# LSH attention with a mixture of experts: whole tiles of slots, low parts on GpSimd, doubled heads with bits last, routing in seven parts

## The chip, the cores and the metric

The kernel runs on one core of a Trainium2 chip. The core has a matrix engine (TensorE, "PE" in the profile, with its weight loads shown apart as "PEld"), three engines for elementwise work (VectorE "DVE", ScalarE "ACT", GpSimd "POOL") and SyncE ("SP"), which here issues most transfers. Every engine works through its own instructions strictly in the order in which the program wrote them, and waits on semaphores for what other engines or transfers have to deliver first. The metric is the device time of one launch in microseconds (us), lower is better; the result must agree with the reference.

## The reference, cut to what matters

Two stages follow each other. The first is attention in buckets: 4 batches of 8 heads, 768 positions, 64 features per head. Six projections give six sign bits for each query and each key, and a query sees only the keys whose six bits are the same as its own. The second is a mixture of 8 experts over the 3072 positions (512 features each, 1024 hidden): every position goes to the one expert with the largest gate logit.

Shortened:

```python
q_bucket = np.sum((np.einsum('bhsd,dk->bhsk', q, proj) > 0) * powers, axis=-1)
k_bucket = np.sum((np.einsum('bhsd,dk->bhsk', k, proj) > 0) * powers, axis=-1)
mask = q_bucket[:, :, :, None] == k_bucket[:, :, None, :]
scores = np.where(mask, scale * np.matmul(q, k.transpose(0, 1, 3, 2)), -1000000000.0)
attn = np.exp(scores - np.max(scores, axis=-1, keepdims=True))
attn = attn / (np.sum(attn, axis=-1, keepdims=True) + 1e-09)
x = np.matmul(attn, v).transpose(0, 2, 1, 3).reshape(B * S, H * D)
...
logits = x @ w_gate
expert_idx = np.argmax(logits, axis=1)
gate_w = softmax(logits)[np.arange(N), expert_idx]
...
h = np.maximum(x_sorted[lo:hi] @ w1[e], 0.0)
y_sorted[lo:hi] = h @ w2[e]
...
return gate_w[:, None] * y
```

## The kernel before, in words

**Order.** No planner is at work (`manual_schedule`): each engine's instructions stand in the order in which the Python code emits them. Moving a line in the code moves it in the queue of its engine.

**Attention.** The 32 heads are taken in 16 pairs; a pair has twelve units of 128 queries by 768 keys (`unit`), so there are 192 units. The main loop runs over rounds `c`, two units per round and six rounds per pair, and is a pipeline. In round `c` TensorE does the value matmuls of round c-5 (`pv`, L339), twelve transposes of exponentials of round c-2 (`trans`, L307) and the score matmuls of round c (`score`, L271 and L273). ScalarE takes the exponentials of round c-1 (`expo`, L288) and evacuates most transposes (L329). VectorE evacuates some (L327) and takes the maxima of the scores (L278 to L280), on which the next exponentials depend.

**Scores with the mask in them.** `qk` tiles hold four planes of a head: plane 1 the rounded keys, plane 3 their low part, planes 0 and 2 the queries rounded, and 64 rows of plane 0 the queries' low part; sixteen rows of planes 2 and 3 hold the sign bits, scaled so that equal buckets add a large constant. A score is a sum of two matmuls per half of the keys, first the one of 80 rows with low parts and bits (L271), then the one of 128 rows (L273). Each head stands twice, so it is loaded into both halves of the 128 partitions (`load_x`, two transfers of 64 rows). For later pairs GpSimd splits the heads (`split`, L175 to L182), 12 pieces spread over the rounds of the pair before, and makes the bits (`lsh_bits`, L234 and L236), which go through a table in DRAM into the sixteen rows (`mask`). For the first two heads this has a form of its own: `lsh_first` (projection, L214), `split_first` (L191 and on) with copies on ScalarE, VectorE and GpSimd, and `bits_first` on VectorE (L234 and L236).

**Routing.** When the four pairs of a batch are through, `route` takes one half batch (384 positions, tiles of 128 x 24): the largest logit, the one-hot of the first expert that has it, ranks by matmuls with a triangle of ones (L421 to L426), and the slot of each position. It is a generator with ten pauses; in each round `go` runs three or two of the parts. `scatter` then writes the rows with indirect transfers of GpSimd to their slots in DRAM (L449). For the last batch the routing stands among the first expert's matmuls.

**Experts.** `pick_first` finds the expert with the most rows once three batches are counted, `rank_all` orders the others. The loads go in phases: the first expert in two halves of 256 slots, then experts with room for 456, 432, 408, 396, 384, 372 and 354 slots; rows beyond that go to a loop at the end. `rows` loads the slots of a phase in tiles of up to 128 (the last one shorter: 72, 48, 24, 12, 128, 116 and 98 rows), `xt` transposes four feature groups (L664) and splits them into a rounded and a low part (L670 and L671). `chunk_part` does the same for the weights, piece by piece of 128 x 512: for the first expert the copies alternate between GpSimd and VectorE in half of the chunks (L622) and the differences are GpSimd's (L623); for all others ScalarE copies (L625), and the differences alternate between VectorE and GpSimd (L626). `mm1` (L689) makes the hidden layer from three products of rounded and low parts, evicted by ScalarE and VectorE (L693 and L694); `mm2` (L715) or, for up to 384 slots, `yout` (L732) the output; where `mm2` is used, `yout` transposes it back (L739). VectorE weighs the rows (L741) and GpSimd scatters them to the output (L743). The weights and rows of the next phase are prepared while the present one is computed.

Of the kernel before, what the change touches and what calls it, by code (L numbers as in the profile page):

```python
# [7 lines left out]
F32 = mybir.dt.float32  # L8
# [42 lines left out]
def lsh_attention_moe(ctx, tc, qk, v, proj, wg, w1, w2, out):  # L51
# [32 lines left out]

    ones = const.tile([128, 128], BF16, name="ones")
# [10 lines left out]
    nc.sync.dma_start(wgt, wg)  # L96

    p = ps.tile([128, 512], F32, name="o")
    for _ in range(WARM):
        nc.tensor.matmul(p, ones, ones[:, None, :].to_broadcast([128, 4, 128]), start=True, stop=True)  # L100
# [83 lines left out]
    def split_first(h, half):  # L184
# [80 lines left out]
    def score(i):  # L265
# [4 lines left out]
        for a in range(2):  # L270
            nc.tensor.matmul(p[:, a, :HALF], k[0:80, 2, c], k[0:80, 3, a * HALF:(a + 1) * HALF], start=True, stop=False)  # L271
        for a in range(2):
            nc.tensor.matmul(p[:, a, :HALF], k[:, 0, c], k[:, 1, a * HALF:(a + 1) * HALF], start=False, stop=True)  # L273
# [121 lines left out]
    def route(b, hf):  # L395

        l = wk.tile([128, 2, 3, E], F32, name="rl")
# [7 lines left out]
        yield  # L405
        nc.vector.tensor_reduce(mx, lg, axis=AX.X, op=OP.max)
        yield
        nc.vector.tensor_tensor(eq, lg, bc(mx), op=OP.is_equal)
        yield
        nc.vector.tensor_tensor(eq, eq, dsc, op=OP.mult)  # L410
# [4 lines left out]
        nc.vector.tensor_tensor(oh, dsc, bc(fi), op=OP.is_equal)  # L415
        yield
        nc.vector.tensor_tensor(lg, lg, bc(mx), op=OP.subtract)
# [14 lines left out]
        nc.vector.tensor_tensor(pb, pb, oh, op=OP.mult)  # L432
# [4 lines left out]
        yield  # L437
        nc.vector.tensor_reduce(f[:, 2], ex, axis=AX.X, op=OP.add)
        yield
        nc.vector.reciprocal(XR[b, hf][:, :, GC], f[:, 2])  # L440
        SL[b, hf] = slot

# [29 lines left out]
    def pick_first():  # L472
        k = keys("key0")
        t = const.tile([128, 4], F32, name="pf")
# [300 lines left out]
    for c in range(NC + 2):  # L775
# [42 lines left out]
        for q, n in routes:  # L818
            go(q, n)
# [199 lines left out]
```

## Time and profile before

| quantity | value |
|---|---|
| time, median of 3 runs | 808.83 us (808.76 to 809.11) |
| time of the profiled execution | 808.29 us |
| its span in the trace | 806.5 us |
| instructions | 14075 |
| exponentials on ScalarE (L288) | 192, of 991 ns |
| maxima on VectorE (L278) | 192, of 952 ns |
| moved by transfers | 114.45 MB, 142 GB/s on average |

The profiled execution is one launch; its span runs from the first to the last thing that the hardware profiler recorded. In a row of the timeline stand the start in microseconds from the start of the span, the busy time, the engine, the line, the operation, the output and input by their names in the program, their shapes, how many instructions the row holds, and in brackets the idle time of the engine before the row with what ended it. In a row by stretches stand the stretch, its length, and then, for PE, PEld, DVE, ACT and POOL, the busy microseconds with the number of instructions, and at the end the granted clock of TensorE, the DMA share and GB/s. In a row of groups stand busy time and mean nanoseconds, and after a bar the idle time before and its releaser. Rows of the chain of waits give the time at which a step began, how long it lasted, engine, output and line.

### The profile page before, as it was taken

Reading aid. Unit: us, or ns where it says so; the run is one execution under the profiler, and the core shown is the slowest. Engines: PE = TensorE matmul, PEld = TensorE weight load, DVE = VectorE, ACT = ScalarE, POOL = GpSimd, SP = SyncE. Lnnn points to the kernel's source line nnn. Section 1 sums busy time; section 2 is a strip of 40 time slices with the busy share of each in tenths; the row PEclk is TensorE's granted clock in tenths of the full one; section 3 lists DMA queues with packets and bytes.
Section 4 is the critical chain, followed back from the end, with each engine's and each line's share of the span. In section 5 each row is a group of like instructions: output and inputs, shape, how many; then the busy total and the mean of one; then the engine's idle time right before and its main releaser. Section 6 shows DMA issues by size and latency. Waiting matters only on the chain.

```text
span 806.5 us, 14075 instructions
## 1 busy us (share of the span) xinstructions
PE 786.3 (97%) x4942; PEld 614.6 (76%) x4942; DVE 524.2 (65%) x1222; ACT 441.7 (55%) x879; POOL 431.1 (53%) x523
## 2 busy tenths in 40 slices
PE   7999999999999999999999989999999999999996
PEld 3767776677667766777667758988999999989894
DVE  6777777897777887778877854472564744445331
ACT  3766776766667766676666731443334343434310
POOL 5976467486756668745769263342333434345311
PEclk6999999999999999999999999999999999999999
DMA  9769963265346336433445113844444445545200
GB/s 228 187 173 282 312 176 98 67 194 160 81 119 158 95 108 202 98 79 98 130 112 164 68 53 136 270 143 161 129 146 150 147 131 175 173 154 189 86 10 35
DMA packets 47248, 114.45 MB, mean 142 GB/s; under 512 B 8265, under 2 KB 12233, under 8 KB 47176
## 3 DMA queue, kind: packets, MB, share of 16 engines
q1 hardware_dynamic: 40504, 97.18, 41.6%
q0 software_dynamic: 6672, 16.35, 6.7%
q8 instruction: 40, 0.66, 0.3%
q14 instruction: 32, 0.26, 0.1%
HBM read 87.50 MB, written 26.51 MB: 141 GB/s over the span
## 4 chain that ended last, share of the span: by engine, by line
PE 85%; DVE 5%; issue 5%; ACT 1%; DMA 1%; POOL 1%; SPq 0%; DVEq 0%; POOLq 0%; ACTq 0%
PE o L339 16%; PE t L307 15%; PE t L689 14%; PE t L715 9%; PE s L271 8%; PE s L273 8%; PE s L732 7%; DVE m L278 2%; PE t L373 2%; PE t L229 2%; PE t L356 1%; PE s L689 1%; ACT e L288 1%; PE s L739 1%; DMA xd<-in_qk_dram 1%
## 5 line engine op out<-in xcount | busy, mean ns | idle before, releaser
L288 ACT ACTIVATE e<-s,m 128x768 f32<-128x768 f32 x192 | 190.2, 991 | 130.1 <-DVE m L280 127.8
L278 DVE TENSOR_REDUCE m<-s 128x1 f32<-128x768 f32 x192 | 182.8, 952 | 62.8 <-PE s L273 54.4
L307 PE MATMUL t<-ident,e 128*128 128x128 f32 x1152 | 148.2, 278 | 1.2 <-ACT pt L329 1.0
L307 PEld LDWEIGHTS t<-ident,e 128*128 128x128 f32 x1152 | 125.4, 141 | 31.3 <-DVE m L280 10.2
L339 PE MATMUL o<-pt,vt 128*64 128x384 f32 x768 | 145.9, 502 | 0.0
L689 PE MATMUL t<-xh,w 128*128 128x456 f32 (+6 forms) x672 | 127.1, 346 | 1.1 <-DVE hh L694 1.1
L626 POOL TENSOR_TENSOR w<-raw,w 128x512 fp32r<-128x512 f32 x56 | 71.9, 1289 | 96.3 <-ACT w L625 96.1
L689 PEld LDWEIGHTS t<-xh,w 128*128 128x128 f32 x672 | 119.1, 188 | 4.4 <-DVE hh L694 1.5
L329 ACT ACTIVATE pt<-t 128x512 f32<-128x512 f32 (+1 forms) x194 | 103.6, 591 | 1.9 <-PE t L307 1.9
L339 PEld LDWEIGHTS o<-pt,vt 128*64 128x64 f32 x768 | 47.0, 137 | 59.1 <-issue 55.2
L626 DVE TENSOR_TENSOR w<-raw,w 128x512 fp32r<-128x512 f32 x56 | 55.9, 1002 | 55.0 <-ACT w L625 50.3
L743 POOL DMA_INDIRECT out_dram<-y,ix x27 | 31.3, 1159 | 92.0 <-DVE y L741 78.6
L715 PE MATMUL t<-hh,w 128*128 128x456 f32 (+3 forms) x384 | 78.9, 359 | 0.0
L327 DVE COPY pt<-t 128x512 f32<-128x512 f32 (+1 forms) x97 | 66.0, 682 | 16.2 <-PE t L307 13.8
L693 ACT ACTIVATE hh<-t 128x256 fp32r<-128x256 f32 (+7 forms) x64 | 31.4, 490 | 79.4 <-PE t L689 79.4
L715 PEld LDWEIGHTS t<-hh,w 128*128 128x128 f32 x384 | 69.8, 188 | 2.8
L694 DVE SCALAR_TENSOR_TENSOR hh<-t,hh 128x256 fp32r<-128x256 f32 (+7 forms) x64 | 35.4, 554 | 50.3 <-ACT hh L693 48.9
L625 ACT ACTIVATE w<-raw 128x512 fp32r<-128x512 f32 x112 | 66.3, 623 | 0.0
L732 PE MATMUL s<-w,hh 128*128 128x512 f32 (+2 forms) x264 | 64.5, 398 | 0.0
L271 PE MATMUL s<-qk 80*128 80x384 f32 x192 | 55.9, 372 | 3.2 <-ACT e L288 3.2
L234 POOL TENSOR_SCALAR bits<-bits 64x384 f32<-64x384 f32 x15 | 22.6, 1510 | 63.6 <-ACT bits L240 63.6
L732 PEld LDWEIGHTS s<-w,hh 128*128 128x128 f32 (+2 forms) x264 | 47.8, 185 | 11.3
(206 smaller groups left out, 1124.6 us busy)
## 6 DMA issues: line engine op xcount, KB each, us to landing
raw<-in_w_dram SPq DMA_DIRECT2D x64, 512.0 KB, 3.7
xd<-in_qk_dram SPq DMA_DIRECT2D x36, 384.0 KB, 5.4
xhe<-in_qk_dram SPq DMA_DIRECT2D x15, 768.0 KB, 8.6
w<-in_qk_dram SPq DMA_DIRECT2D x28, 384.0 KB, 5.4
sorted_rows<-xr SPq DMA_DIRECT2D x8, 1156.0 KB, 14.5
vt<-in_v_dram SPq DMA_DIRECT2D x16, 384.0 KB, 3.3
xg<-sorted_rows SPq DMA_DIRECT2D x19, 289.0 KB, 4.6
masks<-bits SPq DMA_DIRECT2D x15, 192.0 KB, 1.9
```

What stands on the lines that cost most here:

```text
L271: nc.tensor.matmul(p[:, a, :HALF], k[0:80, 2, c], k[0:80, 3, a * HALF:(a + 1) * HALF], start=True, stop=False)
L278: nc.vector.tensor_reduce(m[:, 0:1], p[:, :, :HALF], axis=AX.XY, op=OP.max)
L288: nc.scalar.activation(e, p[:, :, :HALF], AF.Exp, bias=m[:, 2:3], scale=m[:, 1:2], accum_out=SM[g, hf][:, t, s:s + 1])
L307: nc.tensor.transpose(p[:, x * 128:(x + 1) * 128], e[w][:, kt // 3, (kt % 3) * 128:(kt % 3) * 128 + 128], ident)
L327: nc.vector.tensor_copy(o, x)
L329: nc.scalar.activation(o, x, AF.Copy)
L339: nc.tensor.matmul(p[s * 64:(s + 1) * 64, :HALF], VT[g][:, kt, s, :], PT[u][:, s, kt, :], start=(kt == 0), stop=(kt == NT - 1))
L625: nc.scalar.activation(w[:, 0, a], r, AF.Copy)
L626: (nc.vector if a % 2 else nc.gpsimd).tensor_tensor(w[:, 1, a], r, w[:, 0, a], op=OP.subtract)
L689: nc.tensor.matmul(p[:, :c], w[:, a, d, fs], x[:, b, d, :c], start=(k == 0), stop=(k == 11))
L715: nc.tensor.matmul(p[:, :c], w[:, a, f % 4, ms], h[b][:, f, :c], start=(k == 0), stop=(k == 23))
L732: nc.tensor.matmul(p[:pw], HH[n][b][:, f, i:i + pw], w[:, a, f % 4], start=(k == 0), stop=(k == 23))
```

## The change

It has seven parts.

1. *Start.* A second array, in which each head stands twice, is made on the host; `load_x` brings a head with one transfer of 128 rows. The first head is loaded ahead of everything, the projection through ScalarE's queue, and the first values and the gate weights come after the loads of heads 2 and 3.
2. *Warming.* 3, 3 and 9 further matmuls without a use stand among the first ones.
3. *First scores.* The copies of `split_first` come ahead of its differences; VectorE takes the first head's queries' difference, GpSimd all differences of keys. One bits operation of head 1 comes earlier. For the first four units the matmul with low parts and bits comes second.
4. *Routing.* `route` has seven parts, two per round, at two places of a round. Comparisons are written as a difference and a comparison with zero. For the first three batches those and the products are GpSimd's. For the last batch the second half's end, the scatter and the second load of rows stand in the middle of a matmul group of the first expert (`third`).
5. *First expert.* `pick_first` has pauses and is spread over three rounds; its weights are loaded two rounds later than before. In the last two rounds `xt` comes ahead of the weights.
6. *Weights.* All copies for the first expert and all differences are GpSimd's.
7. *Tiles.* `rows`, `tokens` and `xt` take whole tiles of 128 slots, and `yout` transposes up to 72 columns where a tile was shorter.

```diff
-        nc.sync.dma_start(x[0:64], qk[h])
-        nc.sync.dma_start(x[64:128], qk[h])
+        nc.sync.dma_start(x, qk2[h])
...
+    load_x(0)
+    pj = const.tile([128, 32], F32, name="pj")
+    nc.scalar.dma_start(pj, proj)
+    load_x(1)
...
-    load_x(0)
-    pj = const.tile([128, 32], F32, name="pj")
-    nc.sync.dma_start(pj, proj)
-    load_x(1)
-    load_v(0)
...
+    def warmth(p, n):
+
+        for _ in range(n):
+            nc.tensor.matmul(p, ones, ones[:, None, :].to_broadcast([128, 4, 128]), start=True, stop=True)
...
         copy(t[:, 0, c], x[:, c])
-        nc.gpsimd.tensor_tensor(t[64:128, 0, c], x[64:128, c], t[64:128, 0, c], op=OP.subtract)
         copy(t[0:80, 2, c], x[0:80, c])
+        (nc.gpsimd if h or half else nc.vector).tensor_tensor(t[64:128, 0, c], x[64:128, c], t[64:128, 0, c],
+                                                              op=OP.subtract)
         if half == 0:
             for a in range(2):
-                (nc.gpsimd if a or h else nc.vector).tensor_tensor(
+                nc.gpsimd.tensor_tensor(
...
+        for low in ((False, True) if i < 4 else (True, False)):
+            for a in range(2):
+                n = slice(a * HALF, (a + 1) * HALF)
+                if low:
+                    nc.tensor.matmul(p[:, a, :HALF], k[0:80, 2, c], k[0:80, 3, n], start=i >= 4, stop=i < 4)
+                else:
+                    nc.tensor.matmul(p[:, a, :HALF], k[:, 0, c], k[:, 1, n], start=i < 4, stop=i >= 4)
...
+        eng = nc.gpsimd if b < B - 1 else nc.vector
...
-        nc.vector.tensor_tensor(eq, lg, bc(mx), op=OP.is_equal)
-        yield
-        nc.vector.tensor_tensor(eq, eq, dsc, op=OP.mult)
+        eng.tensor_tensor(lg, lg, bc(mx), op=OP.subtract)
+        eng.tensor_scalar(eq, lg, 0.0, None, op0=OP.is_equal)
+        eng.tensor_tensor(eq, eq, dsc, op=OP.mult)
...
-        nc.vector.tensor_tensor(oh, dsc, bc(fi), op=OP.is_equal)
-        yield
-        nc.vector.tensor_tensor(lg, lg, bc(mx), op=OP.subtract)
+        eng.tensor_tensor(eq, dsc, bc(fi), op=OP.subtract)
+        eng.tensor_scalar(oh, eq, 0.0, None, op0=OP.is_equal)
...
-        nc.vector.tensor_tensor(pb, pb, oh, op=OP.mult)
+        eng.tensor_tensor(pb, pb, oh, op=OP.mult)
...
-            (nc.vector if a % 2 and c > 1 else nc.gpsimd).tensor_copy(w[:, 0, a], r)
+            nc.gpsimd.tensor_copy(w[:, 0, a], r)
...
-            (nc.vector if a % 2 else nc.gpsimd).tensor_tensor(w[:, 1, a], r, w[:, 0, a], op=OP.subtract)
+            nc.gpsimd.tensor_tensor(w[:, 1, a], r, w[:, 0, a], op=OP.subtract)
...
-            nc.sync.dma_start(XG[n][:pw, j], xsv[bass.ds(EV[r], 1), o + i:o + i + pw].rearrange("o p w -> p (o w)"))
+            nc.sync.dma_start(XG[n][:, j], xsv[bass.ds(EV[r], 1), o + i:o + i + 128].rearrange("o p w -> p (o w)"))
...
-            nc.tensor.transpose(p[:, i:i + pw], heads(XG[n][:pw, j], d), ident[0:pw, 0:pw])
+            nc.tensor.transpose(p[:, j * 128:(j + 1) * 128], heads(XG[n][:, j], d), ident)
...
+            yw = max(pw, min(128, CAPS[1] - i))
             for m in range(4):
-                nc.tensor.transpose(p[:pw, m * 128:(m + 1) * 128], YT[n][:, m, i:i + pw], ident)
+                nc.tensor.transpose(p[:yw, m * 128:(m + 1) * 128], YT[n][:, m, i:i + yw], ident)
...
     lsh_first(0)
+    warmth(ps.tile([128, 512], F32, name="t", bufs=3), 3)
     split_first(0, 0)
...
     split_first(1, 0)
+    bits_first(1, 0)
+    warmth(ps.tile([128, 512], F32, name="t", bufs=3), 3)
 
     load_pair(1)
     load_x(2)
     load_x(3)
+    load_v(0)
+    nc.sync.dma_start(wgt, wg)
...
-        for q, n in routes:
-            go(q, n)
+        for q in routes:
+            next(q, None)
+        if c in (NC - 13, NC - 11, NC - 10):
+            next(pick)
...
-                for a in (0, 2, 3):
+                for a in (2, 3):
                     bits_first(1, a)
+                warmth(ps.tile([128, 512], F32, name="t", bufs=3), 9)
...
+            for w in routes:
+                next(w, None)
...
-        if c == NC - 11:
-            pick_first()
+        if c == NC - 9:
+            next(pick, None)
             raw_load(0, 0)
             raw_load(0, 1)
         if c == NC - 6:
             rows(0)
+        if c >= NC - 2:
+            xt(0, c - (NC - 2))
         if c >= NC - 6:
             weights((1, 1, 1, 2, 1, 2, 3, 3)[c - NC + 6])
-        if c >= NC - 2:
-            xt(0, c - (NC - 2))
...
+    def third():
+        go(last[1], 3)
+        scatter(B - 1, 1)
+        rows(1)
 
     mm1(0, 2, second)
-
     mm1(0, 3)
-    go(last[1], 9)
-    scatter(B - 1, 1)
-    rows(1)
-    for f in range(4, 8):
+    mm1(0, 4, third)
+    for f in range(5, 8):
         mm1(0, f)
```

More of the change, by code (lines that the diff above doesn't have):

```diff
@@ L89, in lsh_attention_moe @@
     nc.scalar.activation(warm, warm, AF.Exp, bias=0.0, scale=1.0)
-    load_x(0)
-    pj = const.tile([128, 32], F32, name="pj")
-    nc.sync.dma_start(pj, proj)
-    load_x(1)
-    load_v(0)
     wgt = const.tile([128, NP, 32], F32, name="wgt")
[L96 to L100, printed above, removed]
+    def warmth(p, n):
+        for _ in range(n):
+            nc.tensor.matmul(p, ones, ones[:, None, :].to_broadcast([128, 4, 128]), start=True, stop=True)
+    warmth(ps.tile([128, 512], F32, name="o"), WARM)
     def iota(shape, pattern, name, base=0, cm=0):
@@ L269, in score @@
         c = slice((3 * hf + t) * 128, (3 * hf + t) * 128 + 128)
[L270 to L273, printed above, removed]
+        for low in ((False, True) if i < 4 else (True, False)):
[5 more added lines that the diff above has]
+                    nc.tensor.matmul(p[:, a, :HALF], k[:, 0, c], k[:, 1, n], start=i < 4, stop=i >= 4)
         SC[i] = p
@@ L473, in pick_first @@
         k = keys("key0")
+        yield
         t = const.tile([128, 4], F32, name="pf")
@@ L649, in tokens @@
         IX[n] = moe.tile([128, 4], I32, name="ix", bufs=3)
-        for j, m, pw in full_and_rest(c):
-            nc.vector.tensor_copy(IX[n][:pw, j:m], XG[n][:pw, j:m, GC + 1].bitcast(I32))
+        t = len(tiles_of(c))
+        nc.vector.tensor_copy(IX[n][:, :t], XG[n][:, :t, GC + 1].bitcast(I32))
     def heads(x, d):
@@ L662, in xt @@
         p = ps.tile([128, 512], F32, name="t", bufs=3) if d % 2 or n == 0 else ps.tile([128, 512], F32, name="o")
-        for j, (i, pw) in enumerate(tiles_of(c)):
-            nc.tensor.transpose(p[:, i:i + pw], heads(XG[n][:pw, j], d), ident[0:pw, 0:pw])
+        t = len(tiles_of(c))
+        for j in range(t):
+            nc.tensor.transpose(p[:, j * 128:(j + 1) * 128], heads(XG[n][:, j], d), ident)
         if d == 0:
             GT[n] = moe.tile([128, 4], F32, name="gate", bufs=3)
-            for j, m, pw in full_and_rest(c):
-                nc.vector.tensor_copy(GT[n][:pw, j:m], XG[n][:pw, j:m, GC])
+            nc.vector.tensor_copy(GT[n][:, :t], XG[n][:, :t, GC])
             tokens(n)
@@ L760, in lsh_attention_moe @@
     load_x(3)
+    load_v(0)
+    nc.sync.dma_start(wgt, wg)
     NC = NU // 2
-    routes, parts = [], list(range(16))
+    routes, parts, pick = [], list(range(16)), pick_first()
     def weights(n):
@@ L842, in lsh_attention_moe @@
             b, q = divmod(c - 24, 24)
+            for w in routes:
+                next(w, None)
             if q == 3:
-                routes.append((route(b, 0), 3))
+                routes.append(route(b, 0))
             if q == 7:
-                routes.append((route(b, 1), 2))
+                routes[:] = [route(b, 1)]
                 scatter(b, 0)
             if q == 13:
+                routes.clear()
                 scatter(b, 1)
-        if c == NC - 11:
-            pick_first()
+        if c == NC - 9:
+            next(pick, None)
             raw_load(0, 0)
@@ L871, in lsh_attention_moe @@
     last = [route(B - 1, 0), route(B - 1, 1)]
-    go(last[0], 7)
+    go(last[0], 4)
     pv(u, 4)
@@ L878, in lsh_attention_moe @@
     lgt_ev(u, lgt(u), False)
-    go(last[0], 10)
+    go(last[0], 3)
     scatter(B - 1, 0)
```

18 lines of the change are left out of this document (7 added, 11 removed).

## The prediction

> **What bounds the kernel now.** I read the page first: its busy times, then its chain of waits.
>
> ```profile
> span 806.5 us, 14075 instructions
> PE 786.3 (97%) x4942; PEld 614.6 (76%) x4942; DVE 524.2 (65%) x1222; ACT 441.7 (55%) x879; POOL 431.1 (53%) x523
> PE 85%; DVE 5%; issue 5%; ACT 1%; DMA 1%; POOL 1%; SPq 0%; DVEq 0%; POOLq 0%; ACTq 0%
> ```
>
> TensorE works for 97% of the span and carries 85% of the chain. So another engine's work is worth something only where TensorE stops, is slowed, or streams something that need not be streamed. I therefore looked, in the timeline, for the places where TensorE has an idle time in brackets, and found five kinds of loss: the start, routing inside attention, one hole at 421 us, one at 475 us, one at 540 us. A sixth is hidden in the transposes of short tiles. Next came the table by stretches, whose last three columns are granted clock, DMA share and GB/s:
>
> ```profile
> 9.00:10.00 1.00, 1.00 (x8) 0.16 (x8) 0.97 (x2) 0.00 (x0) 0.77 (x1) 0.50 0.98 224
> 12.00:13.00 1.00, 1.00 (x5) 0.94 (x3) 0.79 (x1) 0.37 (x1) 0.92 (x1) 0.50 1.08 412
> 21.00:24.00 3.00, 3.00 (x22) 2.96 (x21) 1.48 (x4) 1.23 (x4) 2.90 (x3) 0.91 1.02 229
> 476.00:478.00 2.00, 2.00 (x12) 0.73 (x12) 0.59 (x2) 0.66 (x2) 2.00 (x3) 0.50 0.44 166
> ```
>
> While half-height head loads run, the queue moves 224 GB/s; while the 128-row loads of values and pairs run, 412. The clock is at half until about 21.5 us, and again at 476 to 478.
>
> **Start: 4.5 us.** These timeline rows carry it:
>
> ```profile
> 6.99 0.94 ACT L191 ACTIVATE qk<-xd 128x384 fp32r<-128x384 f32 x2 [4.73 <-DMA xd<-in_qk_dram]
> 10.60 0.94 ACT L191 ACTIVATE qk<-xd 128x384 fp32r<-128x384 f32 x2 [2.67 <-DMA xd<-in_qk_dram]
> 9.41 1.38 DVE L236 TENSOR_SCALAR qk<-t,thr,mul 16x384 fp32r<-16x384 f32 x2
> 12.21 0.96 DVE L278 TENSOR_REDUCE m<-s 128x1 f32<-128x768 f32 x1 [1.42 <-PE s L273]
> 16.80 0.96 DVE L278 TENSOR_REDUCE m<-s 128x1 f32<-128x768 f32 x1
> 19.23 0.83 POOL L175 CAST w<-w 128x768 fp32r<-128x768 f32 x1
> 19.52 2.48 PE L307 MATMUL t<-ident,e 128*128 128x128 f32 x12
> 25.56 0.59 PE L271 MATMUL s<-qk 80*128 80x384 f32 x2 [0.83 <-ACT e L288]
> 36.32 1.00 POOL L182 TENSOR_TENSOR w<-w,w 64x384 fp32r<-64x384 f32 x1
> 38.68 0.59 PE L271 MATMUL s<-w 80*128 80x384 f32 x2
> ```
>
> The doubled array lets one 128-row load bring a head. A head is 786 KB: 3.5 us at 224 GB/s, 1.9 at 412, so head 0 is there at 5.4 instead of 6.99, and head 1 (twice the bytes; 7.0 us or 3.8) at about 7.3 instead of 10.60. VectorE's bits of head 0 end at 10.79, 3.8 us after landing. That chain keeps its length (the subtraction that VectorE gives to GpSimd is replaced by one of 64 rows that it takes over), so the bits end at 9.2. Today four matmuls follow the bits before the first maximum can start at 12.21. With bits last, two follow, and at full clock they take some 0.5 us: maximum at 9.8, a gain of 2.4. One of head 1's bits now comes ahead of the maxima (half of a 1.38 pair is 0.7; I take 0.55, since the row-wise kind is shorter), so the third maximum moves from 16.80 by 2.95. The 18 extra warming matmuls stand where TensorE waits anyway. They should keep the granted clock up. Then the last score (0.7 after the third maximum's bits at 13.85), the next pair's projection (about 0.9) and the first twelve transposes (1.46, as in the chain rows below, not 2.48) end at about 17.0, not 22.0. After that TensorE waits on exponentials (25.56), whose inputs moved by as much as the scores. GpSimd is the limit from the other side: it starts on the next pair (19.23) when head 1 is split, some 3.2 earlier, and its last split would end at 37.3 - 3.2 = 34.1, while TensorE would want that pair at 38.68 - 4.5 = 34.2. So the bounds are 3.0 (VectorE and GpSimd) and 5.1 (TensorE). I take 4.5, nearer to the TensorE rows, since both other engines wait for it from 22 us on. Without full clock only about 2.0 remain. The projection load on ScalarE's queue shows in no row; landing like the other start loads it is hidden, and as late as head 1 it would cost 1.5. The values load, now behind the loads of heads 2 and 3, is first needed after 31 us.
>
> **Routing: 1.0 us.** The chain of waits gives the length of four groups of six rounds by their transposes:
>
> ```profile
> 132.14 1.46 PE t L307 x12
> 160.80 1.46 PE t L307 x12
> 190.07 1.46 PE t L307 x12
> 218.40 1.46 PE t L307 x12
> L408 DVE TENSOR_TENSOR rl<-rl,rf 128x24 f32<-128x24 f32 x8 | 4.9, 610 | 0.2
> ```
>
> A plain group takes 28.33 (190.07 to 218.40). The group with a batch's first route takes 28.66, which I take to be that route's matmuls alone (0.33); the one with the second 29.27, so 0.94, 0.6 more than its matmuls. Three such groups lose 1.8 us to VectorE: its 24-element comparison takes 610 ns on average, too long for so few elements. GpSimd now does these. Each result crosses between engines, and VectorE and TensorE would wait in order (behind them: the maxima, then exponentials, then scores) if GpSimd were late. By the places in the program it reaches a part about when VectorE does. Bounds 1.7 gained to 1.5 lost; I take 1.0.
>
> **Hole at 421: 1.0 us.**
>
> ```profile
> 419.12 0.16 DVE L466 TENSOR_TENSOR key<-base,base 128x8 f32<-128x8 f32 x1
> 420.94 0.66 PE L307 MATMUL t<-ident,e 128*128 128x128 f32 x4 [1.01 <-ACT pt L329]
> ```
>
> The first expert's choice is eight small VectorE operations in one round, and the evacuations queued behind them hold the transposes for 1.01 us. Spread over three rounds they fit in VectorE's idle time; bounds 0.5 and 1.2. The weight load starts two rounds (some 9 us) later and is still used only three rounds after that, so it stays hidden; SyncE queues nothing urgent behind it.
>
> **Hole at 475: 3.2 us.**
>
> ```profile
> 474.23 0.86 DVE L622 CAST w<-raw 128x512 fp32r<-128x512 f32 x1 [1.68 <-POOL w L623]
> 475.01 0.41 DVE L671 TENSOR_TENSOR xhe<-t,xhe 128x256 fp32r<-128x256 f32 x1
> 475.48 0.80 PE L689 MATMUL s<-xhe,w 128*128 128x256 f32 x2 [1.89 <-DVE xhe L671]
> 476.79 3.83 PE L339 MATMUL o<-pt,vt 128*64 128x384 f32 x16
> 183.17 1.44 PE o L339 x8
> ```
>
> VectorE's weight copy waits 1.68 us for GpSimd, and the token split that TensorE needs stands behind it. The change gives the copies to GpSimd and puts the split first: the hole goes, but for about 0.3. The clock is at half after it (the 476 row above): sixteen value matmuls take 3.83, where eight at full clock take 1.44 (the last row, from the chain), so 0.95 less; and the 1.3 us between the hole's end and them would be 0.65. Together 1.6 + 1.6 = 3.2. GpSimd's copies and differences of the last eight parts (0.63 + 1.28 each) then end near 480, as now, ahead of their use after 490. The bounds are 1.6 and 3.5.
>
> The Trainium skill ("TensorE: Matmul & The Clock Gate", Why this matters for your kernels) allows idle gaps up to about 3 us without loss of clock. Here 1.89 us were enough; by the page the half clock would have another cause, and the sum would lose 1.6.
>
> **Hole at 540: 1.2 us.**
>
> ```profile
> 532.80 6.41 DVE L626 TENSOR_TENSOR w<-raw,w 128x512 fp32r<-128x512 f32 x2
> 533.03 5.03 POOL L626 TENSOR_TENSOR w<-raw,w 128x512 fp32r<-128x512 f32 x4
> 539.81 12.76 PE L689 MATMUL t<-xh,w 128*128 128x456 f32 x60 [1.12 <-DVE hh L694]
> L626 POOL TENSOR_TENSOR w<-raw,w 128x512 fp32r<-128x512 f32 x56 | 71.9, 1289 | 96.3 <-ACT w L625 96.1
> L743 POOL DMA_INDIRECT out_dram<-y,ix x27 | 31.3, 1159 | 92.0 <-DVE y L741 78.6
> ```
>
> Two VectorE differences take 6.41 us while GpSimd does four, and the hidden-layer evictions behind them stop TensorE. With all of them on GpSimd that is gone. GpSimd gets 56 x 1.289 = 72 us more. An expert then costs it 16 x 1.29 + 4 x 1.16 = 25 us, against 34 to 44 of TensorE (only the second half of the first expert, 24.5 us, is as short). There the queue behind the last scatter ends near 541, and the weights are first used after 552.57.
>
> The Trainium skill ("GPSIMD Engine Reference", 4.1 Engine selection) says not to give two-input elementwise work to GpSimd, which is about twice as slow. Per piece the trace agrees, 1289 ns; where the cover holds it is free.
>
> **Short tiles: 2.8 us.**
>
> ```profile
> 527.35 0.56 PE L664 MATMUL o<-ident,xg 128*128 128x128 f32 x4
> 527.70 3.05 PE L732 MATMUL s<-w,hh 128*128 128x512 f32 x12
> 557.36 0.68 PE L664 MATMUL o<-ident,xg 128*128 128x128 f32 x4
> 557.97 5.22 PE L715 MATMUL t<-hh,w 128*128 128x456 f32 x24
> 641.48 0.65 PE L664 MATMUL o<-ident,xg 128*128 128x128 f32 x4
> 642.05 1.19 PE L715 MATMUL t<-hh,w 128*128 128x408 f32 x5
> ```
>
> Four transposes whose last has 72 rows take 0.35 us until the next matmul starts; with 48 rows 0.61, with 12 rows 0.57. The short ones cost 0.22 to 0.26 more though they stream less. Whole tiles should all take 0.35. Three experts (48, 24, 12 rows) with four such sets each: 4 x (0.26 + 0.23 + 0.22) = 2.8. The 72-, 116- and 98-row tiles gain nothing. If a whole tile paid for its columns instead, the term would be -0.5. Output transposes of at most 72 columns stream 128 anyway: nothing.
>
> **Sum.** 4.5 + 1.0 + 1.0 + 3.2 + 1.2 + 2.8 = 13.7. The profiled execution took 808.29 (its span and 1.8 around it), so 794.6; the median of the runs shown lies 0.5 higher, and I forecast 795.1.
>
> **Rivals.** *The start is worth half*: the clock falls back or GpSimd's splits set the pace. For: GpSimd is busy 2.90 of 3 us there; against: its last split has 1.3 us to spare now. 2.25 less gained: 797.4. *The hole at 475 stays*, because the last parts' raw weights land late: 795.1 + 3.2 = 798.3. *Whole tiles cost their columns*, so that the change doesn't do there what it says: 795.1 + 3.3 = 798.4. *GpSimd is late in routing*, slower than before: its parts stand behind splits (1.00 each) and scatters. If in each of six routes the one-hot comes a round of 4.8 us late, of which 1.1 is spare, TensorE loses 6 x 3.7 = 22 at the rank matmuls: 808.8 - 12.7 + 22 = 818. It turns slower than now from 2.1 us lost per route on. For: in-order queue, two handovers per route; against: 53% busy. *GpSimd becomes the bound in the expert stage*: differences moved at 1289 instead of about 680 (DVE alone) cost 56 x 0.61 = 34 if they came onto the path: 795.1 + 34 = 829; it decides once the 11 us of spare before 552.57 are gone. The page on engine selection speaks for it.
>
> **Chances.** Forecast 0.64, its own range 792.5 to 797.5; half a start 0.12; hole stays 0.08; tiles 0.04; late routing 0.05; expert bound 0.03; more gained than summed 0.04. A measurement here tells about 0.2% (1.6 us) from no change. Faster 0.91, same 0.03, slower 0.06. Range 791.5 to 799.5: below by the upper bounds of start, routing and 475 together, above by the rivals at 797 to 798.
>
> **What would show it.** Head 0's first ScalarE copy near 5.4; granted clock 1.00 from 10 us on; transposes of the first round by 15 to 16; no TensorE idle time near 418, 470 or 530 and no half clock in the middle; four transposes always 0.35; plain groups still 28.3. I am wrong if TensorE waits for GpSimd at the rank matmuls or at weights, or if the third maximum is later than 15.

## The result and the profile after

The changed kernel takes 796.17 us (median of 4 runs, 794.86 to 797.72) against 808.8 beside it (808.43 to 809.11): a ratio of 0.9845, 95% interval 0.9822 to 0.9868. The forecast was 795.1. In a second series it took 794.65 (794.53 to 794.99, 5 runs) against 806.26 (805.46 to 808.8): 0.985, interval 0.9831 to 0.9869.

The page of the changed kernel, profiled in an execution of 797.33 us (span, busy times, chain of waits):

```profile
span 795.5 us, 14002 instructions
PE 782.7 (98%) x4957; PEld 613.8 (77%) x4957; DVE 472.5 (59%) x1122; ACT 441.2 (55%) x879; POOL 507.4 (64%) x619
PE 91%; issue 3%; DVE 3%; POOL 1%; ACT 1%; POOLq 0%; DVEq 0%; ACTq 0%
```

VectorE gave 52 us of work away and GpSimd took 76; TensorE now carries 91% of the chain instead of 85%. Behind 30 us no idle time of TensorE ends on GpSimd in this trace.

The four times lie in two pairs, 794.9 and 795.0, 797.3 and 797.7. The cause is at the start, and the first experiment shows it; the median of 796.17 is the middle between the two pairs, and no run lay there. So the gains are given below for three pairs of traces: the traces of record (the profiled execution of before above and the one on this page), the trace of before with that of the changed kernel's lower level, and both at the lower level. Each figure is the difference of the distances between the same two matmuls (the first transposes of a group of rounds, or the first matmul of an expert) in two traces. The figures are rounded one by one, so a column can miss its sum by 0.1.

| stretch | forecast | record to record | before, record, to lower level | lower to lower |
|---|---|---|---|---|
| start, until the third pair of heads | 4.5 | 1.0 | 3.7 | 3.1 |
| routing of three batches | 1.0 | 0.7 | 0.7 | 0.7 |
| choice of the first expert (421) | 1.0 | 1.2 | 1.2 | 1.2 |
| weights and tokens (475) | 3.2 | 3.5 | 3.5 | 1.75 |
| last batch's routing | none | 0.3 | 0.3 | 0.3 |
| low parts (540) | 1.2 | 1.4 | 1.4 | 1.4 |
| tiles of 48, 24 and 12 rows | 2.8 | 3.1 | 3.1 | 3.1 |
| behind the last output | 0 | -0.3 | -0.3 | -0.3 |
| sum (difference of the spans) | 13.7 | 11.0 | 13.7 | 11.35 |

The 0.3 behind the last output lie between the last scatter and the end of the program; no run tells why.

### The profile page after: what moved, and what is told of

Read it like the earlier page. It is cut to its first block, busy times and chain, and to the rows that moved or that the text cites. A ratio compares the mean times of both kernels' runs of the same rounds, so it can differ in the third digit from the quotient of the medians.

```text
span 795.5 us, 14002 instructions
## 1 busy us (share of the span) xinstructions
PE 782.7 (98%) x4957; PEld 613.8 (77%) x4957; DVE 472.5 (59%) x1122; ACT 441.2 (55%) x879; POOL 507.4 (64%) x619
## 4 chain that ended last, share of the span: by engine, by line
PE 91%; issue 3%; DVE 3%; POOL 1%; ACT 1%; POOLq 0%; DVEq 0%; ACTq 0%
PE o L344 17%; PE t L312 16%; PE t L690 15%; PE t L716 9%; PE s L276 8%; PE s L278 8%; PE s L733 7%; PE t L378 2%; DVE m L283 2%; PE t L230 1%; PE t L361 1%; PE s L690 1%; PE s L742 1%; PE t L666 1%; PE o L666 1%
## 5 line engine op out<-in xcount | busy, mean ns | idle before, releaser
L632 POOL TENSOR_TENSOR w<-raw,w 128x512 fp32r<-128x512 f32 x112 | 142.3, 1294 | 44.6 <-ACT w L631 43.1
L746 POOL DMA_INDIRECT out_dram<-y,ix x27 | 26.9, 995 | 73.5 <-DVE y L744 32.8
L276 PE MATMUL s<-w 80*128 80x384 f32 x192 | 53.4, 359 | 0.0
```

The source lines that it names most:

```text
L276: nc.tensor.matmul(p[:, a, :HALF], k[0:80, 2, c], k[0:80, 3, n], start=i >= 4, stop=i < 4)
L632: nc.gpsimd.tensor_tensor(w[:, 1, a], r, w[:, 0, a], op=OP.subtract)
```

## The experiments

They ran in three series of four kernels, each series on another chip; the kernel before took 806.26, 806.38 and 809.25 us beside them. The changed kernel itself ran in the first series alone, and all times are held against its 794.65 there; where less than one us is at stake, the distances of the marks (the matmuls of the table above) in the traces carry the verdict.

### The changed kernel again

> The changed kernel as it is, again. In the run on record its four times lay at 794.9, 795.0, 797.3 and 797.7, and the profiled one (797.3) had pairs of score matmuls of 0.84 us until 13.5 us and of 0.52 later. Theory (clock at the start): the two levels are two positions of the clock's windows of 3.41 us against the start of the program. Then the times again fall in two groups 2.3 to 2.8 apart and nothing between, and if the profile is of the lower group its matmuls are at 0.52 us per pair from 10.5 us or earlier, the first transposes start near 15.8 instead of 18.16, and everything after has the same distances. Rival (the difference arises later, for example in a weight load or a scatter): the first transposes start at 18.2 in both groups, and the lower group gains its 2.5 us at one place in the middle.

Measured: 794.53 to 794.99 in five runs, all at the lower level, so no second group showed here. Its profile can be held against that of record. Rows of the timeline, first of record, then of this run:

```profile
10.61 1.20 PE L278 MATMUL s<-qk 128*128 128x384 f32 x2
12.25 0.84 PE L278 MATMUL s<-qk 128*128 128x384 f32 x2
12.49 0.96 DVE L283 TENSOR_REDUCE m<-s 128x1 f32<-128x768 f32 x1 [2.03 <-PE s L276]
16.51 0.59 PE L278 MATMUL s<-qk 128*128 128x384 f32 x2
16.63 0.96 DVE L283 TENSOR_REDUCE m<-s 128x1 f32<-128x768 f32 x1
18.16 0.66 PE L312 MATMUL t<-ident,e 128*128 128x128 f32 x4
```

```profile
5.12 0.62 DVE L200 CAST qk<-xd 128x384 fp32r<-128x384 f32 x2 [2.31 <-DMA xd<-in_qk_dram]
8.64 0.70 PE L278 MATMUL s<-qk 128*128 128x384 f32 x2
9.56 0.51 PE L278 MATMUL s<-qk 128*128 128x384 f32 x2
9.76 0.96 DVE L283 TENSOR_REDUCE m<-s 128x1 f32<-128x768 f32 x1
13.90 0.96 DVE L283 TENSOR_REDUCE m<-s 128x1 f32<-128x768 f32 x1
15.42 0.66 PE L312 MATMUL t<-ident,e 128*128 128x128 f32 x4
```

The same two matmuls take 0.84 us at 12.25 in the one and 0.51 at 9.56 in the other. The first transposes are 2.74 us apart, and every later mark is 2.63 to 2.74 apart, down to the last expert. So the whole difference of the two levels arises at the start, from the clock. The traces record when the granted clock changes; before its first record a trace shows the clock as full, and only the matmuls tell. The records, in us from the start of the span, without the last one of each trace, a half clock behind the last matmuls:

```
kernel before, record      full 4.45, half 7.87, full 21.52, half 475.49, full 478.91
kernel before, again       full 20.17
changed kernel, record     full 13.81
changed kernel, again      full 6.33
without further warming    full 4.60, half 8.02, full 18.26
```

Every step between two changes is a multiple of 3.413 us: the chip decides once per window. The windows do not begin with the program: 13.81 and 6.33 lie 7.48 apart, which is no multiple. The Trainium skill ("TensorE: Matmul & The Clock Gate", Part 1) says that the window is 3413 ns long and free-running; the traces agree.

### Without the further warming

```diff
     lsh_first(0)
-    warmth(ps.tile([128, 512], F32, name="t", bufs=3), 3)
...
     bits_first(1, 0)
-    warmth(ps.tile([128, 512], F32, name="t", bufs=3), 3)
...
-                warmth(ps.tile([128, 512], F32, name="t", bufs=3), 9)
```

> The changed kernel without the 3, 3 and 9 further warming matmuls. Theory (they stand on the path): at half clock a group of three takes 1.3 us, and the second one lies between the end of head 1's projection (9.8) and the first score (10.6). Without them head 1's projection starts near 7.2, the first score near 9.3 when VectorE's bits are done, the first maximum at 11.2 instead of 12.49, and the time is 0.5 to 1.5 below the changed kernel's. Rival (they hold the clock): without them the clock stays at half until 18 to 21 us, as in the kernel before, pairs of score matmuls stay at 0.84, the first transposes start at 18.5 to 19.5 and the time is 798 to 799.

Measured: 795.75 (795.13 to 795.9, 4 runs), 1.1 above the changed kernel of the same series. Its timeline:

```profile
7.30 0.86 PE L215 MATMUL o<-xd,pj 64*32 64x384 f32 x8 [1.03 <-DMA xd<-in_qk_dram]
9.86 0.84 PE L278 MATMUL s<-qk 128*128 128x384 f32 x2
14.41 0.96 DVE L283 TENSOR_REDUCE m<-s 128x1 f32<-128x768 f32 x1 [0.20 <-PE s L276]
17.11 2.07 PE L312 MATMUL t<-ident,e 128*128 128x128 f32 x12
```

The rival has the mechanism: with 1.0 us idle ahead of 7.30 the clock falls to half at 8.02 and stays there until 18.26, and the first transposes come 1.7 later than in the run above. Its sizes, worked out from the trace of record, do not fit: it had the first transposes at 18.5 to 19.5 and the time at 798 to 799. The warming keeps the clock, for 1.0 us. The other side shows against the trace of record, where the clock is at half until 13.81 in spite of the warming: without it the first transposes stand at 17.11 instead of 18.16, and the span is 1.7 shorter (793.8 against 795.5). There the warming may stand in the way (the second group ahead of the score at 10.61); since the windows of the two traces begin at different places, that is not measured by itself.

### Head 1's projection behind the first score

```diff
-    lsh_first(1)
     split_first(1, 0)
-    bits_first(1, 0)
...
                 score(i)
+            if i == 0:
+                lsh_first(1)
             if i == 1:
-                for a in (2, 3):
+                for a in (0, 2, 3):
```

> Head 1's projection moved from ahead of the first score to behind it, and its first bits to the other two behind the second score; the warming matmuls stay. Theory (order: the first score waits for head 1's projection and for warming, not for its own bits, which end at 9.25): the first score starts near 9.4 instead of 10.6, the first maximum near 10.7 to 11.2 instead of 12.49, the first transposes 1.0 to 2.0 earlier, the time 1 to 2 below the changed kernel's. It also gives TensorE full-size work in the place of the small projection, so under the clock theory the granted clock rises one window (3.41) earlier and the upper of the two groups becomes rarer. Rival (VectorE sets the pace: its bits of head 1 come before the third maximum): the third maximum stays at 16.6, and the time within 0.5 of the changed kernel's.

Measured: 795.62 (795.38 to 796.4, 4 runs), 1.0 slower (0.8 by the marks). VectorE's maxima and the first transposes:

```profile
9.71 0.96 DVE L283 TENSOR_REDUCE m<-s 128x1 f32<-128x768 f32 x1 [0.54 <-PE s L276]
14.68 0.96 DVE L283 TENSOR_REDUCE m<-s 128x1 f32<-128x768 f32 x1
15.86 0.65 PE L312 MATMUL t<-ident,e 128*128 128x128 f32 x4
```

Its clock is full from 6.37, as in the changed kernel again, so this is a comparison at the same clock. The first maximum is where it was (9.76), and the third moved from 13.90 to 14.68, since all three bits operations of head 1 now stand ahead of it on VectorE. At full clock VectorE sets the pace of the start; the theory of the order fell. How the order does at half clock, from which the expectation was worked out, was not measured.

### The old start

```diff
-        nc.sync.dma_start(x, qk2[h])
+        nc.sync.dma_start(x[0:64], qk[h])
+        nc.sync.dma_start(x[64:128], qk[h])
...
+    load_x(0)
+    pj = const.tile([128, 32], F32, name="pj")
+    nc.sync.dma_start(pj, proj)
+    load_x(1)
+    load_v(0)
...
-        for low in ((False, True) if i < 4 else (True, False)):
+        for low in (True, False):
```

The old order of `split_first` and of the bits is back too, and the further warming is out.

> The changed kernel with the start of the kernel before: half-height head loads, the old order of loads, copies, differences and bits, low parts and bits first in all scores, no further warming. Everything behind it as changed. If the whole start is worth what the profiled run shows (first transposes 1.36 earlier, 1.04 after the first pairs), the time is 798.0 to 799.0, in one group. If the start is worth what was forecast (4.5), the time is 799.5 to 801.5. Rival (the start gains nothing in the end, since GpSimd's splits for the next pairs set the pace): the same as the changed kernel, 795 to 797.5.

Measured: 798.05 (797.14 to 798.29, 5 runs), 3.4 above the changed kernel of the same series. The time is where the first case put it (798 to 799), but that case took the changed kernel's upper level; beside its lower level the start is worth 3.4 (3.7 by the marks), between the 1.04 of the record's trace and the 4.5 of the forecast. Its timeline:

```profile
7.12 0.85 PE L217 MATMUL t<-xd,pj 64*32 64x384 f32 x8 [1.90 <-DMA pj<-in_proj_dram]
19.31 0.90 PE L314 MATMUL t<-ident,e 128*128 128x128 f32 x3
```

TensorE idles 1.90 us for the projection's load, the clock is at half from 8.19 to 21.85, and the first transposes start at 19.31 instead of 15.42. The kernel without further warming loses 1.0 of these 3.7, so loads and orders are worth the other 2.7, compared without warming; which of them brings how much was not taken apart.

### The kernel before again

> The kernel before as it is, again. Beside the first four experiments its times lay at 805.5 to 806.5 and 808.2 to 808.8, where the first runs had all been 808.4 to 809.1. Theory (grid of clock windows): the lower level is again another position of the windows of 3.41 us. Then a profile of the lower level shows the first transposes some 1 to 2.5 us earlier than 19.52, or no half-clock window behind the hole near 475, and the same distances everywhere else; one of the upper level repeats the trace of before within 0.3 us at every stage. Rival (the levels come from transfers): the difference of about 2.5 lies at a wait for a load, with the clock's records unchanged.

Measured: 806.23 (805.4 to 808.67, 10 runs); the profile is of a run of 805.94. The hole near 475, and the granted clock (third column from the end) behind it:

```profile
474.68 0.50 PE L689 MATMUL s<-xhe,w 128*128 128x256 f32 x2 [1.68 <-DVE xhe L671]
475.46 2.80 PE L339 MATMUL o<-pt,vt 128*64 128x384 f32 x16
475.00:477.00 2.00, 2.00 (x18) 0.92 (x18) 0.15 (x1) 0.64 (x2) 1.77 (x3) 1.00 0.62 219
```

The idle time is there, 1.68 us, and no half clock follows: the sixteen value matmuls take 2.80, not 3.83. Against the trace of record 0.6 is gained at the start and 1.77 at this place, nothing anywhere else. By the window grid of this trace (20.17 and multiples of 3.413) a boundary lies at 474.14, so 1.14 us of the idle time fall in one window and 0.54 in the next. In the trace of record the window from 472.08 to 475.49 holds all of the 1.89. The theory of the grid holds for both kernels.

### Short tiles back

```diff
-            nc.sync.dma_start(XG[n][:, j], xsv[bass.ds(EV[r], 1), o + i:o + i + 128].rearrange("o p w -> p (o w)"))
+            nc.sync.dma_start(XG[n][:pw, j], xsv[bass.ds(EV[r], 1), o + i:o + i + pw].rearrange("o p w -> p (o w)"))
...
-            nc.tensor.transpose(p[:, j * 128:(j + 1) * 128], heads(XG[n][:, j], d), ident)
+            nc.tensor.transpose(p[:, i:i + pw], heads(XG[n][:pw, j], d), ident[0:pw, 0:pw])
```

The output transposes of short tiles, and VectorE's copies of gates and places, are as before too.

> The changed kernel with the last tiles of a phase short again (72, 48, 24, 12, 128, 116 and 98 rows loaded and transposed, as before). The changed kernel gained 1.18, 1.00 and 0.93 us on the stretches in which the tiles of 48, 24 and 12 rows are transposed. Theory (the short transposes cost more than whole ones): four transposes take 0.61, 0.59 and 0.57 us again instead of 0.35, the distance from the start of the second matmul phase's expert of 432 slots to that of 396 slots grows by these 2.7 to 3.2 us, and the time is 2.7 to 3.2 above the changed kernel's at the same level (797.4 at the lower one). Rival (GpSimd's taking over the differences gave these gains): no more than 0.3.

Measured: 797.71 (797.68 to 797.81, 4 runs), 3.1 above the 794.65 of the changed kernel. The marks lose 1.18, 1.0 and 0.93 across the three tiles and no more than 0.1 elsewhere. One set in the changed kernel again, and the same with a last tile of 48 rows:

```profile
546.52 0.60 PE L666 MATMUL o<-ident,xg 128*128 128x128 f32 x4
546.87 5.18 PE L716 MATMUL t<-hh,w 128*128 128x456 f32 x24
```

```profile
546.45 0.68 PE L670 MATMUL o<-ident,xg 128*128 128x128 f32 x4
547.05 5.22 PE L721 MATMUL t<-hh,w 128*128 128x456 f32 x24
```

From the first transpose to the next matmul it is 0.35 and 0.60 us. Twelve such sets make 2.8; the other 0.3 are small steps between them (0.03 or less each) and were not traced further.

### The first expert's copies back on VectorE

```diff
-            nc.gpsimd.tensor_copy(w[:, 0, a], r)
+            (nc.vector if a % 2 and c > 1 else nc.gpsimd).tensor_copy(w[:, 0, a], r)
```

> The changed kernel with the first expert's weight copies (second half of its chunks) alternating between VectorE and GpSimd again; the token transposes stay ahead of the weights. The changed kernel has no hole near 475 us and gained 3.5 there. Theory (the copies on VectorE that wait for GpSimd were the cause, the order helps only for the last round's own copies): VectorE's copies of the rounds before still wait for GpSimd with the tokens' differences behind them, and 1 to 2 us of TensorE idle time come back, with a half-clock window if the idle time is over 1.5: time 1.0 to 3.5 above the changed kernel's at the same level. Rival (the order alone does it): within 0.3.

Measured: 798.42 (797.21 to 798.82, 4 runs), 3.8 above (3.9 by the marks). Rows of VectorE, GpSimd and TensorE, and the clock behind them:

```profile
473.20 0.59 DVE L628 CAST w<-raw 128x512 fp32r<-128x512 f32 x1 [2.05 <-DMA raw<-in_w_dram]
474.05 0.59 DVE L390 TENSOR_TENSOR xr<-t,r 128x432 f32<-128x432 f32 x1
475.70 1.18 DVE L414 TENSOR_SCALAR rl<-rl 128x24 f32<-128x24 f32 x1
474.34 2.50 POOL L629 TENSOR_TENSOR w<-raw,w 128x512 fp32r<-128x512 f32 x2
477.80 0.19 PE L425 MATMUL t<-oh,tri 128*128 128x24 bf16 x1 [2.33 <-DVE oh L421]
479.00:481.00 2.00, 2.00 (x11) 2.00 (x11) 0.97 (x4) 0.00 (x0) 0.96 (x1) 0.50 0.00 0
```

VectorE's copy waits 2.05 us for a raw weight load, and with the tokens out of its way the last batch's routing is what stands behind it. The token operation ahead of it starts 2.0 later than in the changed kernel again:

```profile
472.05 0.61 DVE L390 TENSOR_TENSOR xr<-t,r 128x432 f32<-128x432 f32 x1 [2.75 <-PE t L380]
```

Another 0.4 come from VectorE's operations behind it (L414 takes 1.18 beside GpSimd's differences, 0.18 elsewhere). TensorE idles 2.33, inside one window of this trace, and the clock is halved for the next. The copies on VectorE are the cause, but not by the way of the theory: they wait for a load and not for GpSimd, the routing stands behind them and not the tokens, and 2.33 and 3.8 lie above the 1 to 2 and 1.0 to 3.5 expected.

### The order of tokens and weights back

```diff
-        if c >= NC - 2:
-            xt(0, c - (NC - 2))
         if c >= NC - 6:
             weights((1, 1, 1, 2, 1, 2, 3, 3)[c - NC + 6])
+        if c >= NC - 2:
+            xt(0, c - (NC - 2))
```

> The changed kernel with the weights ahead of the token transposes in the last two rounds again; all copies stay on GpSimd. Theory (copies were the cause): VectorE and ScalarE hold nothing of the weights in these rounds, so the order cannot matter: within 0.2 of the changed kernel, no hole near 475. Rival (the order alone does it): the hole returns, 1.5 to 3.5 slower.

Measured: 794.77 (794.55 to 794.95, 4 runs), against 794.65. No hole, all marks within 0.1. Once the copies are GpSimd's, the order is worth nothing; and by the run before, the order alone does not close the hole.

### Low parts back on both engines

```diff
-            nc.gpsimd.tensor_tensor(w[:, 1, a], r, w[:, 0, a], op=OP.subtract)
+            (nc.vector if a % 2 else nc.gpsimd).tensor_tensor(w[:, 1, a], r, w[:, 0, a], op=OP.subtract)
```

> The changed kernel with the other experts' low parts alternating between VectorE and GpSimd again. Theory (two differences on VectorE together with GpSimd's hold the hidden layer's evictions): TensorE stops for about 1.1 us behind the first full expert's matmuls again, near 524 to 526 us, the distance across that expert's first matmul phase grows by 1.3 to 1.4, and the time is 1.0 to 1.6 above the changed kernel's at the same level (796.0 at the lower one). Rival (the differences on VectorE are harmless once the first expert's copies and the tiles have been changed): within 0.3.

Measured: 796.17 (796.02 to 796.51, 4 runs), 1.5 above, with the hole back (1.4 across that expert's first matmul phase, 0.1 behind it). It ends at 530.47, later than the 524 to 526 expected:

```profile
523.51 6.36 DVE L632 TENSOR_TENSOR w<-raw,w 128x512 fp32r<-128x512 f32 x2 [0.17 <-ACT w L631]
523.69 5.03 POOL L632 TENSOR_TENSOR w<-raw,w 128x512 fp32r<-128x512 f32 x4
530.47 1.72 PE L690 MATMUL t<-xh,w 128*128 128x456 f32 x7 [1.12 <-DVE hh L695]
```

Taken apart, VectorE's first difference lasts 5.76 us and ends 0.55 behind the fourth of GpSimd; its second takes 0.68. The engines did not share: VectorE stood until GpSimd had done all four, though its record starts 0.18 ahead of the first of them.

### The choice of the first expert in one round

```diff
-        if c in (NC - 13, NC - 11, NC - 10):
-            next(pick)
...
-        if c == NC - 9:
-            next(pick, None)
+        if c == NC - 11:
+            for _ in pick:
+                pass
```

> The changed kernel with the choice of the first expert in one round again, and its first weights loaded two rounds earlier, as before. Theory: the round behind the choice takes 6.0 us again instead of 4.8, with 1.0 us of TensorE idle time near 415; in return the 0.42 us of idle time near 405 go and the round there takes 5.1 instead of 5.7, since the first of the three parts is what lies ahead of the evacuations in that round. So the time is 0.5 to 0.8 above the changed kernel's at the same level. Rival (the routing on GpSimd makes the idle time near 405): it stays, and the time is 1.0 to 1.3 above.

Measured: 795.32 (795.15 to 795.41, 4 runs), 0.7 above. TensorE in this kernel, and in the changed one again:

```profile
415.81 0.66 PE L312 MATMUL t<-ident,e 128*128 128x128 f32 x4 [1.02 <-ACT e L293]
```

```profile
405.50 0.66 PE L312 MATMUL t<-ident,e 128*128 128x128 f32 x4 [0.41 <-DVE xr L390]
```

As expected, 1.2 are lost in the round behind the choice, and 0.6 are won where the first of the three parts had stood, ahead of a token operation (L390). So the spreading brought 1.2 and gave 0.6 of it back. Much of the 0.6 may come from the first operation of the choice, which was not tested by itself. In the changed kernel again it takes 0.91 beside a difference of GpSimd; with the choice in one round it takes 0.16:

```profile
400.95 0.91 DVE L469 TENSOR_TENSOR key<-base,base 128x8 f32<-128x8 f32 x1
400.83 1.01 POOL L182 TENSOR_TENSOR qk<-xd,qk 64x384 fp32r<-64x384 f32 x1
```

```profile
413.99 0.16 DVE L469 TENSOR_TENSOR key<-base,base 128x8 f32<-128x8 f32 x1
```

### Routing on VectorE in seven parts

```diff
-        eng = nc.gpsimd if b < B - 1 else nc.vector
+        eng = nc.vector
```

> The changed kernel with all of the routing's small operations on VectorE, in the new seven parts. The groups of rounds with a batch's second route took 29.26 and 29.14 us before and 28.82 and 28.66 after. Theory (VectorE's slow comparisons of 24 elements cost it): 29.1 to 29.6 per such group, so 1.0 to 2.0 in three batches, time 795.6 to 796.6 at the lower level. Rival (the spreading over seven parts at two places of a round brought the gain): 28.6 to 28.9 again, and the time within 0.3 of the changed kernel's.

Measured: 814.3 (812.97 to 816.76, 6 runs) against 809.25 beside it (807.52 to 812.23): slower than the kernel before, ratio 1.0063, interval 1.0039 to 1.0086. Its marks lose 19.0 us in three batches against the changed kernel again, ten times what was expected. Rows of VectorE, GpSimd and TensorE, and VectorE's group:

```profile
163.16 2.70 DVE L413 TENSOR_TENSOR rl<-rl,rf 128x24 f32<-128x24 f32 x1
163.88 1.94 POOL L179 TENSOR_TENSOR qk<-xd,qk 80x384 fp32r<-80x384 f32 x2
167.15 0.66 PE L312 MATMUL t<-ident,e 128*128 128x128 f32 x4 [3.11 <-DVE xr L390]
L413 DVE TENSOR_TENSOR rl<-rl,rf 128x24 f32<-128x24 f32 x8 | 9.0, 1126 | 0.1
```

The same operation on GpSimd in the changed kernel again:

```profile
162.66 0.22 POOL L413 TENSOR_TENSOR rl<-rl,rf 128x24 f32<-128x24 f32 x1
```

A subtraction of 24 elements per partition stands 2.70 us on VectorE. It starts while GpSimd runs a copy and ends 0.05 behind the second of two differences that follow without a pause. The token operation behind it, on which the transposes' buffers hang, holds TensorE for 3.11 us. That costs a half-clock window each time as well (records at 167.86, 287.33 and 406.80). In the kernel before, the comparisons stood at other places of the round and met GpSimd for a shorter time: the longest three took 1.30 to 1.35 and also end 0.05 behind an operation of GpSimd. One of them:

```profile
166.98 1.35 DVE L408 TENSOR_TENSOR rl<-rl,rf 128x24 f32<-128x24 f32 x1
166.32 1.97 POOL L179 TENSOR_TENSOR qk<-xd,qk 80x384 fp32r<-80x384 f32 x2
```

So the seven parts, with their new forms of the comparisons, are a loss on VectorE; the 0.7 belongs to the parts together with GpSimd.

### A version with two places mended

```diff
-        if c in (NC - 13, NC - 11, NC - 10):
+        if c in (NC - 12, NC - 11, NC - 10):
...
+        if lsh and not g:
+            lsh_ev(1)
         if c and c <= NC:
             expo(2 * c - 2)
-        if lsh:
+        if lsh and g:
             lsh_ev(g + 1)
```

> A version meant to be better than both: the first part of the choice of the first expert comes one round later (behind the last part of the third batch's routing, not in the same round as a token evacuation), and for the second pair of heads ScalarE evacuates the projection ahead of the third and fourth exponential. Theory: the idle time near 405 (0.41) goes and the round there takes 5.1 instead of 5.7, 0.4 to 0.6 gained in that group; of the 0.83 us of idle time near 17, most goes at that place, but TensorE waits for exponentials until 27 us, so 0 to 0.5 is left after the first pair. Time 0.4 to 1.0 below the changed kernel's, 793.6 to 794.2 at the lower level. Rival: the later exponential is waited for, the first pair takes as much longer, and only the 0.4 to 0.6 stay.

Measured: 793.94 (793.84 to 794.04, 5 runs), 0.981 of the kernel before beside it (interval 0.9785 to 0.9833), 0.7 below the 794.65 of the changed kernel. The span is 792.1 against 792.8. The idle time near 405 is gone (0.57 gained there). Near 17 the changed kernel again has the first of these rows, and this version the second:

```profile
16.91 1.09 PE L312 MATMUL t<-ident,e 128*128 128x128 f32 x8 [0.83 <-ACT bits L241]
```

```profile
17.20 0.66 PE L312 MATMUL t<-ident,e 128*128 128x128 f32 x4 [0.48 <-DVE qk L235]
```

0.34 stay behind the first pair, and 0.13 are given back among the experts.

## Why the prediction was right, point by point

**The level.** 795.1 lies between the two levels of the changed kernel. The sum of 13.7 equals the distance from before's trace of record to the lower level (806.54 to 792.84). Beside each other at the lower level the kernels are 11.35 apart, since the forecast was made from a trace of before whose windows lay unluckily at 475. That the sum fits to 0.1 is luck: in that column the start is 0.8, routing 0.3 and the end 0.3 short, and the other rows make up 1.3. The median of record hangs on how many of its four runs fell on which level.

**Start: mis-sized.** Head 0 there at 5.4, the first maximum at 9.8 and the third at 13.85 came out at 5.1, 9.76 and 13.90 at the lower level, but in the trace of record at 5.25, 12.49 and 16.63. The step that failed there is "they should keep the granted clock up": in that grid the clock was half until 13.81, and 1.0 was gained, less than the 2.0 that the text kept for that case. So one of its own signs of being wrong, a third maximum later than 15, came in that trace, and the first transposes stood at 18.16, not by 15 to 16. Two figures were misread: there are 15 further warming matmuls, not 18, and the clock before was full from 4.45 to 7.87, not at half throughout. With the clock full, 3.7 were gained where 4.5 was taken. VectorE sets the pace, nearer to the lower of the two bounds (3.0), as head 1's late projection showed; and the first twelve transposes, forecast to end at 17.0, end at 18.0, with 0.83 of idle time among them that ScalarE ends.

**Routing: right in size, short in reason.** 0.7 in three batches and 0.3 in the last, which the text did not name. The 610 ns per comparison were the sign of VectorE standing while GpSimd works, and the danger lay opposite to where the rival put it: GpSimd was never late, but VectorE beside it loses 19.

**Hole at 421: right**, 1.2 for 1.0, with 0.6 lost where the first of its parts stands. That round lies in the stretch of the routing term, which would be 1.3 without it. That the parts fit in VectorE's idle time did not hold for the first of them.

**Hole at 475: right.** 1.6 for the idle time and 1.6 for the clock were forecast; 1.75 are gained where no half clock follows the hole before, and 3.5 where one does. The price of the clock hangs on the grid; the prediction had 1.6 as a lower bound, but put the clock whole into the sum. Of its two means, copies on GpSimd and the split first, the copies alone close the hole.

**Hole at 540 and short tiles: right**, 1.4 for 1.2 and 3.1 for 2.8, each given back when its edit was undone (1.5 and 3.1). The prediction gave no reason for the 6.41 us of VectorE's two differences; it was standing until GpSimd was through.

**Rivals.** GpSimd is late in routing, GpSimd bounds the experts, whole tiles cost their columns, the hole stays: none came. The clock's half of the rival on the start came in the trace of record, at 797.3 where 797.4 was worked out; but the start gained 1.0 there and not 2.25, so the close fit of the time is luck.

## What to carry to other kernels

Work that is handed from one elementwise engine to another is worth what stops behind it in the giver's queue, not its own duration: 0.2 us operations held TensorE for 3.1, and a copy that waits for a load stood behind 2.0 of the 2.3 in another run. Before a small operation is put on VectorE, look at what GpSimd does in those microseconds. And before a term is written for the clock, find the windows of 3.41 us in the trace: the same idle time costs or does not cost a half-clock window by where it falls, so such a term belongs in the range and not in the sum.

## What was not expected of the hardware

**The clock goes by idle time inside one window.** An idle time of 1.89 us inside one window was followed by 3.41 us at half clock, and so were 2.33, 2.72 and 3.11 of which most lay in one; 1.68 split into 1.14 and 0.54 was not. At the start, a window in which warming alone filled all but some 0.7 us brought full clock (a record at 3.80 in the kernel with the copies on VectorE). In the trace of record the first window had some 0.9 us without a matmul, and the next two were filled by two fifths with projections of 64 rows by 32 columns: none of them brought it. Without the further warming, 1.33 us of idle time in the window from 4.60 to 8.02, beside two such projections, were followed by half clock. With the old start, 1.51 us in the window from 786.43 to 789.85, behind matmuls of 512 columns, were not. That small matmuls count less is an inference from these three traces; no run tested it.

**VectorE stands while GpSimd works without a pause.** Its subtraction of 128 x 24 took 2.70 us beside GpSimd, 0.17 at best; one of 128 x 8 took 0.91 and 0.16; one of 128 x 512 took 5.76 beside four of GpSimd's, 0.68 alone; GpSimd's own took 1.28 to 1.30 each throughout. The Trainium skill ("SBUF — State Buffer", Who interferes with whom) says that the two engines share a port pair under an exclusive lock, and that the later one blocks until the first is done. The traces agree on the block and go further: in the first and the last of these VectorE did not get in between GpSimd's instructions either, as long as these followed without a pause.
